# Equal tile offsets, scaled states on two engines, and products that fill TensorE's waits

## The chip, the cores and the metric

The kernel runs on one core of one Trainium2 chip. The metric is the device time of one execution in microseconds (us); the core has five engines, named as the profile names them: PE (TensorE matmul; PEld is its weight load), DVE (VectorE), ACT (ScalarE), POOL (GpSimd) and SP (SyncE, which here only issues DMAs).

## What is computed

Three stages, each feeding the next, all in float32 at the inputs and outputs:

```python
# gated linear attention, 4 batches x 8 heads, 768 steps, head size 48
for t in range(S):
    state = alpha[:, :, t, :, None] * state + einsum('bhd,bhe->bhde', k[:, :, t], v[:, :, t])
    y[:, :, t] = einsum('bhd,bhde->bhe', q[:, :, t], state)
x = y.transpose(0, 2, 1, 3).reshape(3072, 384)
# first feed-forward, 384 -> 2048 -> 384
h = x @ w_in;  x = (h * cos(h)) @ w_out
# second feed-forward, 384 -> 768 -> 384
h = maximum(maximum(x @ w1, x @ w2), x @ w3);  out = h @ w_out2
```

## The kernel before

The 3072 tokens are cut into six units of 512 (`u`). Attention (`att`) works a unit in four pairs of heads (`p`, processed as `k` = 0 to 3), and cuts 512 steps into eight chunks of 64. In a pair, POOL and DVE scale k and q by running products of alpha; TensorE transposes k (`trans`, L387), multiplies k with q and k with v (`akmm`, L399 and L404); ACT copies the k-q scores out (`a`, L411) and POOL masks them (L412); DVE carries the state from chunk to chunk (`state`, L421 and L423). TensorE then adds two parts into the output: scores by v (L449) and "scaled states" `d` by q (L455). A scaled state is a chunk's state times one column of `g`: in the first unit ACT makes it, one chunk and one head at a time (L430, 14 of them in a pair); in the later units POOL makes it, one head and all eight chunks at a time (L435, 2 in a pair). ACT copies the result out in two halves (L470), and in the first unit TensorE subtracts that rounded copy and ACT writes the remainder (L473, L475).

The first feed-forward, `moe1`, has 96 iterations, 16 blocks of hidden columns for each of six units. Each has 9 products that make h (L497 to L499) and 9 that multiply g into three accumulators (L524 to L526); a product streams 512 columns of a "moving" tile against a 128x128 stationary weight. Every number is held as a high and a low float32r part, so a float32 product takes three. The weights `wih`, `wil`, `woh`, `wol` are unpacked as they arrive: three DVE instructions a block (L310 to L312), one of ACT (L315) and one of POOL (L316). The second feed-forward, `moe2_h` (L574 to L576) and `moe2_o` (L597 to L599), is built of products of the same shape.

The order is not written by hand. Every step is recorded with an engine, an estimated duration, what it reads and writes, and a due time; `Program.order` simulates the engines and takes on each the earliest due step that is ready. Then the steps are issued in that order, each engine running its own list strictly in turn. So the estimated duration of one step can change the order of all.

The tiles lie in SBUF pools. The pool of attention's tiles (`ap`) starts at byte 73,856 of a partition. The pools of the feed-forward weights (`w1p`) and of the second feed-forward's hidden tiles (`np`) grow from the upper end, byte 229,344, downward. In the built program the tiles' first bytes, as remainders of a division by 64, are these:

| tile | before | after |
|---|---|---|
| moving tiles of `moe1`: `xt`, `gh`, `gl` | 0 | 0 |
| its weights `wih`, `wil`, `woh`, `wol` | 32 | 0 |
| `moe2_h`: moving `xt` / weights `w0`..`w2` | 0 / 0 | 0 / 0 |
| `moe2_o`: moving `h2` / weights `wo2` | 32 / 32 | 0 / 0 |
| attention's `kq` / `d` / `v`, `a`, `kt` | 32 / 0 / 0 | 0 / 0 / 0 |

Of the kernel before, what the change touches and what calls it, by code (L numbers as in the profile page):

```python
# [9 lines left out]
F32 = mybir.dt.float32  # L10
# [3 lines left out]
AF = mybir.ActivationFunctionType  # L14
# [4 lines left out]
B, H, S, D = 4, 8, 768, 48  # L19
# [4 lines left out]
P = 128  # L24
C = 64
HB = 512
NC = HB // C
# [4 lines left out]
C1 = C + 1  # L32
AL = NC * C1
# [14 lines left out]


NQ, NG, NRAW, NIN, NV, NGS = 3, 2, 3, 3, 2, 3  # L50
NBANK = 5
LIMIT = {"h": 3, "a": 3, "t": 1, "w": 1, "r": 2, "y": 2, "r0": 4}

# [9 lines left out]
MKP = 1  # L63

DAC = 1


W1E = 10
# [5 lines left out]


WARM, COLD, IDLE = 16, 7.0, 2.5


class Program:
# [15 lines left out]
    def op(self, eng, dur, fn, reads=(), writes=(), due=0.0, nbytes=None, port=False):  # L95
        n = len(self.ops)
        deps = set()
        for k in reads:
            if k in self.last_write:
                deps.add(self.last_write[k])  # L100
        for k in writes:
            if k in self.last_write:
                deps.add(self.last_write[k])
            deps.update(self.readers.get(k, ()))
        for k in writes:
            self.last_write[k] = n
            self.readers[k] = []
        for k in reads:
            self.readers.setdefault(k, []).append(n)
        for k in {*reads, *writes}:  # L110
            if isinstance(k, tuple) and k[0] == "ps":
                self.of_bank.setdefault(k, []).append(n)
        deps.discard(n)
        port = port or (eng == "Pool" and nbytes is None)
        self.ops.append((eng, dur, nbytes, fn, sorted(deps), due, port))
        return n

    def order(self, banks, limit):
        n = len(self.ops)
        left = [len(o[4]) for o in self.ops]  # L120
        users = [[] for _ in range(n)]
        for i, o in enumerate(self.ops):
            for d in o[4]:
                users[d].append(i)
        opens = {}
        bank_of = [[] for _ in range(n)]
        open_left = {}
        for k, v in self.of_bank.items():
            opens.setdefault(min(v), []).append(k)
            open_left[k] = len(v)  # L130
            for i in v:
                bank_of[i].append(k)
        bank_free = [0.0] * banks
        freed_at = {c: [0.0] * limit[c] for c in limit}
        bank_end = {}
        chosen = {}
        engines = sorted({o[0] for o in self.ops})
        free = dict.fromkeys(engines, 0.0)
        waiting = {e: [] for e in engines}
        ready_at = [0.0] * n  # L140
        for i in range(n):
            if not left[i]:
                waiting[self.ops[i][0]].append(i)
        start = [0.0] * n
        dma_free = 0.0
        port_free = 0.0
        cold = COLD
        never = float("inf")

        def single(t):  # L150
            return min(range(banks), key=lambda m: (bank_free[m] > t, bank_free[m], m))

        def ready(i):
            t = ready_at[i]
            need = opens.get(i, ())
            if need:

                t = max(t, sorted(freed_at[need[0][1]])[len(need) - 1], sorted(bank_free)[len(need) - 1])
            if self.ops[i][6]:
                t = max(t, port_free)  # L160
            return t

        for _ in range(n):
            t, e = min((max(free[e], min(map(ready, w))), e) for e, w in waiting.items() if w)
            assert t < never
            i = min((self.ops[j][5], j) for j in waiting[e] if ready(j) <= t)[1]
            waiting[e].remove(i)
            _, dur, nbytes, _, _, _, port = self.ops[i]
            start[i] = t
            if e == "PE":  # L170
                if t - free[e] > IDLE:
                    cold = t + COLD
                dur += min(dur, max(0.0, cold - t) / 2)
            free[e] = t + dur
            end = t + dur
            if port:
                port_free = end
            if nbytes is not None:
                dma_free = max(dma_free, end + (0.65 if e == "SP" else 1.05)) + nbytes / 260e3
                end = dma_free + 0.9  # L180
            for k in opens.get(i, ()):
                f = min(range(limit[k[1]]), key=lambda f: freed_at[k[1]][f])
                m = single(t)
                chosen[k] = m
                bank_end[k] = (m, f, 0.0)
                freed_at[k[1]][f] = never
                bank_free[m] = never
            for k in bank_of[i]:
                m, f, last = bank_end[k]
                last = max(last, end + self.SEM)  # L190
                bank_end[k] = (m, f, last)
                open_left[k] -= 1
                if not open_left[k]:
                    freed_at[k[1]][f] = last
                    bank_free[m] = last
            for u in users[i]:
                lag = self.LAG.get((e, self.ops[u][0]), self.SEM)
                ready_at[u] = max(ready_at[u], end + lag)
                left[u] -= 1
                if not left[u]:  # L200
                    waiting[self.ops[u][0]].append(u)
        self.start = start
        return sorted(range(n), key=lambda i: (start[i], i)), chosen


def act(n, psum=False):
    return (0.05 if psum else 0.095) + 0.00084 * n
# [33 lines left out]
def tile_kernel(ctx, tc, qka, vv, wt, outT):  # L241
# [18 lines left out]
    wi = {n: wp.tile([P, NF1, NR, P], F32R, name=f"wi{n}") for n in "hl"}  # L260
    wo = {n: wp.tile([P, NF1, DM], F32R, name=f"wo{n}") for n in "hl"}

    q_b = [mp.tile([P, HB], F32, name=f"q{i}") for i in range(NQ)]
    gh_b = [mp.tile([P, HB], F32R, name=f"gh{i}") for i in range(NG)]
    gl_b = [mp.tile([P, HB], F32R, name=f"gl{i}") for i in range(NG)]
# [2 lines left out]
    acc = [pp.tile([P, HB], F32, name=f"acc{i}") for i in range(NR)]  # L268
    ps_b = [pp.tile([P, 512], F32, name=f"ps{i}") for i in range(NBANK)]

    one0 = ap.tile([PR, NC, C1], F32, name="one0")
    inv0 = [ap.tile([PR, NC, C1], F32, name=f"inv{i}") for i in range(2)]
    tri = ap.tile([P, 1, C], F32, name="tri")
    al_b = [ap.tile([PR, KO], F32, name=f"al{i}") for i in range(NIN)]
    kq_b = [ap.tile([PR, 2 * HB], F32, name=f"kq{i}") for i in range(NIN)]
    g_b = [ap.tile([PR, AL], F32, name=f"g{i}") for i in range(NGS)]
    v_b = [ap.tile([P, N2, 2, UP], F32, name=f"v{i}") for i in range(NV)]
    kt_b = [ap.tile([P, N2, PR], F32, name=f"kt{i}") for i in range(2)]
    a_b = [ap.tile([P, 2, N2, C], F32, name=f"a{i}") for i in range(2)]
# [57 lines left out]
    def att(u, k, p, t0):  # L337
# [87 lines left out]
        for c in range(NC - 1):  # L425
            op("DVE", 0.2, lambda c=c: state(c), [rk[c % 2], *kgs, (*sk, c)], [(*sk, c + 1)], t0 + 0.25)
            if u < DAC and not firsts[c + 1]:
                for j in range(2):
                    w = slice(UP * j, UP * j + D)
                    op("Act", act(D) + 0.09, lambda c=c, j=j, w=w: se.activation(d[w, j, c + 1], s[w, c + 1], AF.Copy, scale=g[w, c + 1, 0:1]),  # L430
                       [*kgs, (*sk, c + 1)], [(dk, j, c + 1)], t0 + 0.25)
        if u >= DAC:
            for j in range(2):
                w = slice(UP * j, UP * j + D)
                op("Pool", pool(NC * D), lambda j=j, w=w: ge.tensor_tensor(d[w, j], s[w], g[w, :, 0:1].to_broadcast([D, NC, D]), ALU.mult),  # L435
                   [*kgs, *[(*sk, c) for c in range(NC)]], [(dk, j, c) for c in range(NC)], t0 + 0.25)
        elif not firsts[0]:
            for j in range(2):
                w = slice(UP * j, UP * j + D)
                op("Act", act(D) + 0.09, lambda j=j, w=w: se.activation(d[w, j, 0], s[w, 0], AF.Copy, scale=g[w, 0, 0:1]), [*kgs, (*sk, 0)], [(dk, j, 0)], t0 + 0.25)  # L440
        op("DVE", 0.2, lambda: state(NC - 1), [rk[1], *kgs, (*sk, NC - 1)], [(*sk, 0)], t0 + 0.27)

        yks, y = ([("acc", 0), ("acc", 1)], acc[:2]) if u == 0 else psum2("r" if u <= RYS else "y")
# [103 lines left out]
    def open_np():  # L547
        s_w1.close()
        np_ = ctx.enter_context(tc.tile_pool(name="np", bufs=1, side="right"))
        w2t["h2"] = [np_.tile([P, NF2, 2, HB], F32R, name=f"h2_{i}") for i in range(2)]  # L550
        w2t["t"] = [np_.tile([P, HB], F32, name=f"t2_{i}") for i in range(2)]
        w2t["y"] = [np_.tile([P, HB], F32, name=f"y2_{i}") for i in range(2)]
        for n in "hl":
            w2t["o" + n] = np_.tile([P, NF2, DM], F32R, name=f"wo2{n}")

    def x2_in(u, t0):
        n = u % 2
# [131 lines left out]
    build()  # L689
    order, chosen_ = G.order(NBANK, LIMIT)  # L690
    chosen.update(chosen_)
    build()
    with tc.manual_schedule():
        for i in order:
            G.ops[i][3]()


# [62 lines left out]
```

## Time and profile before

| | |
|---|---|
| time, median of 3 runs | 831.05 us (829.34 to 832.0) |
| the profiled execution | 831.06 us, its span 829.3 us |
| busy in the span | PE 805.4, DVE 477.7, ACT 372.5, POOL 189.0 us |
| TensorE's mean granted clock | 0.979 of full |

The span runs from the first to the last profiled instruction. A busy PE is not PE at its peak: matmuls are pipelined, and their recorded durations overlap. The distance from start to start tells the pace.

### The profile page before, as it was taken

The numbers are of one execution on the slowest core, as the hardware profiler recorded it, in microseconds if no ns is written. First come the engines' busy times: TensorE is split into PE (matmuls) and PEld (weight loads), VectorE is DVE, ScalarE is ACT, GpSimd is POOL, SyncE is SP. The second block draws the span as 40 slices with busy tenths as digits, with TensorE's granted clock in tenths as the row PEclk, the third lists the DMA queues.
The fourth block names the chain that finished last, engine by engine and source line by source line (L and its number), as shares of the span: only waits on it lengthen the run. The fifth ranks groups of instructions, "written<-read, shape, count | busy, mean of one in ns | idle before, by whom it ended". The sixth has DMA issues, their size and how long they took to land.

```text
span 829.3 us, 15144 instructions
## 1 busy us (share of the span) xinstructions
PE 805.4 (97%) x6168; PEld 649.1 (78%) x6168; DVE 477.7 (58%) x924; ACT 372.5 (45%) x695; POOL 189.0 (23%) x187
## 2 busy tenths in 40 slices
PE   7689999999999999999999999999999999999998
PEld 6567777878778877887788778888888888888886
DVE  7689999875786577657679954453122222322221
ACT  5865655645555554556466745521121211112121
POOL 6478777621231023102033200110000000000000
PEclk8589999999999999999999999999999999999999
DMA  9446764330242024102224610232020020200001
GB/s 281 137 133 193 208 188 150 117 106 12 73 146 65 1 76 143 43 1 74 65 86 134 238 45 2 104 106 77 26 88 19 22 89 25 77 26 13 13 26 38
DMA packets 26661, 71.86 MB, mean 87 GB/s; under 512 B 3488, under 2 KB 3488, under 8 KB 26592
## 3 DMA queue, kind: packets, MB, share of 16 engines
q1 hardware_dynamic: 26592, 70.90, 26.9%
q8 instruction: 48, 0.79, 0.4%
q14 instruction: 21, 0.17, 0.1%
HBM read 54.37 MB, written 14.16 MB: 83 GB/s over the span
## 4 chain that ended last, share of the span: by engine, by line
PE 84%; DVE 5%; POOL 4%; issue 3%; DMA 2%; ACT 1%; SPq 0%; DVEq 0%; POOLq 0%; ACTq 0%
PE ps L575 9%; PE ps L576 9%; PE ps L574 9%; PE acc L524 8%; PE acc L526 7%; PE ps L497 7%; PE acc L525 7%; PE ps L499 7%; PE ps L498 7%; PE ps L599 3%; PE ps L598 3%; PE ps L597 3%; PE ps L455 2%; PE ps L449 1%; PE ps L399 1%
## 5 line engine op out<-in xcount | busy, mean ns | idle before, releaser
L497 PE MATMUL ps<-xt,wih 128*128 128x512 f32 x288 | 117.7, 409 | 2.8 <-ACT q L506 1.7
L524 PE MATMUL acc<-gh,woh 128*128 128x512 f32 x288 | 117.5, 408 | 0.3 <-DVE yy L534 0.2
L499 PE MATMUL ps<-xt,wil 128*128 128x512 f32 x288 | 115.0, 399 | 1.4 <-POOL wil L316 1.4
L526 PE MATMUL acc<-gl,woh 128*128 128x512 f32 x288 | 114.4, 397 | 0.6 <-DVE gl L519 0.4
L498 PE MATMUL ps<-xt,wih 128*128 128x512 f32 x288 | 114.8, 399 | 0.0
L525 PE MATMUL acc<-gh,wol 128*128 128x512 f32 x288 | 114.0, 396 | 0.0
L504 ACT ACTIVATE q<-ps 128x512 int32<-128x512 f32 x96 | 57.2, 596 | 70.8 <-PE ps L499 70.2
L584 DVE TENSOR_TENSOR ps<-t,ps 128x512 f32<-128x512 f32 x36 | 25.0, 695 | 104.8 <-PE ps L576 104.7
L513 DVE SCALAR_TENSOR_TENSOR ps<-q,ps 128x512 f32<-128x512 f32 x76 | 52.7, 693 | 55.4 <-ACT q L507 55.2
L506 ACT ACTIVATE q<-q 128x512 f32<-128x512 f32 x96 | 60.6, 631 | 50.3 <-DVE q L505 49.6
L505 DVE SCALAR_TENSOR_TENSOR q<-q,ps 128x512 f32<-128x512 int32 x96 | 65.8, 685 | 28.0 <-ACT q L504 24.8
L585 ACT ACTIVATE h<-ps 128x512 fp32r<-128x512 f32 x36 | 21.5, 598 | 113.1 <-DVE ps L584 113.0
L519 DVE TENSOR_TENSOR gl<-ps,gh 128x512 fp32r<-128x512 f32 x76 | 52.1, 685 | 26.4 <-ACT gh L514 26.2
L497 PEld LDWEIGHTS ps<-xt,wih 128*128 128x128 f32 x288 | 54.6, 189 | 16.2 <-ACT q L506 2.2
L499 PEld LDWEIGHTS ps<-xt,wil 128*128 128x128 f32 x288 | 54.6, 190 | 15.3 <-POOL wil L316 2.1
L524 PEld LDWEIGHTS acc<-gh,woh 128*128 128x128 f32 x288 | 54.2, 188 | 15.0 <-DVE yy L534 1.1
L582 DVE TENSOR_TENSOR t<-t,ps 128x512 f32<-128x512 f32 x36 | 24.7, 687 | 71.4 <-PE ps L576 70.7
L526 PEld LDWEIGHTS acc<-gl,woh 128*128 128x128 f32 x288 | 54.2, 188 | 14.6 <-DVE gl L519 0.8
L514 ACT ACTIVATE gh<-ps 128x512 fp32r<-128x512 f32 x76 | 45.3, 597 | 42.8 <-DVE ps L513 39.9
L498 PEld LDWEIGHTS ps<-xt,wih 128*128 128x128 f32 x288 | 54.8, 190 | 11.8
L525 PEld LDWEIGHTS acc<-gh,wol 128*128 128x128 f32 x288 | 54.3, 189 | 11.7
L435 POOL TENSOR_TENSOR d<-s,g 48x384 f32<-48x384 f32 x40 | 34.6, 864 | 122.7 <-DVE s L423 121.1
(122 smaller groups left out, 1595.2 us busy)
## 6 DMA issues: line engine op xcount, KB each, us to landing
raw<-in_wt SPq DMA_DIRECT2D x56, 384.0 KB, 3.4
kq<-in_qka SPq DMA_DIRECT2D x23, 448.0 KB, 4.5
x1d<-yy SPq DMA_DIRECT2D x18, 512.0 KB, 2.8
xt<-x1d SPq DMA_DIRECT2D x18, 512.0 KB, 4.3
v<-in_vv SPq DMA_DIRECT2D x22, 256.0 KB, 3.5
al<-in_qka SPq DMA_DIRECT2D x24, 228.4 KB, 3.0
outT<-y SPq DMA_DIRECT2D x18, 256.0 KB, 2.0
xt<-yy SPq DMA_DIRECT2D x36, 64.0 KB, 2.7
```

Source lines behind the costliest of these rows:

```text
L497: pe.matmul(ps, wi["h"][:, f, cc], xt[:, cc, 0], start=(cc == 0), stop=False)
L498: pe.matmul(ps, wi["h"][:, f, cc], xt[:, cc, 1], start=False, stop=False)
L499: pe.matmul(ps, wi["l"][:, f, cc], xt[:, cc, 0], start=False, stop=(cc == NR - 1))
L504: op("Act", act(HB, True), lambda: se.activation(q.bitcast(I32), ps, AF.Copy, scale=INV2PI), [hk], [qk], m)
L505: op("DVE", dve(HB), lambda: ve.scalar_tensor_tensor(q, q.bitcast(I32), -TWOPI, ps, ALU.mult, ALU.add), [hk], [qk], m)
L506: op("Act", act(HB), lambda: se.activation(q, q, AF.Sin, scale=0.5), (), [qk], m)
L524: pe.matmul(acc[c], oh, gh, start=(f == 0), stop=False)
L525: pe.matmul(acc[c], ol, gh, start=False, stop=False)
L526: pe.matmul(acc[c], oh, gl, start=False, stop=(f == NF1 - 1))
L574: pe.matmul(ps, w2t["h"][m][:, f, cc], xt[:, cc, 0], start=(cc == 0), stop=False)
L575: pe.matmul(ps, w2t["h"][m][:, f, cc], xt[:, cc, 1], start=False, stop=False)
L576: pe.matmul(ps, w2t["l"][m][:, f, cc], xt[:, cc, 0], start=False, stop=(cc == NR - 1))
```

## The change

Three things change. (1) Attention's tiles `one0`, `inv`, `al` and `g` get lines of 544 floats (2,176 bytes) in place of 520 or 522, of which the same part is used as before, and a tile of 88 floats (352 bytes) is added in each of the two pools that grow from the upper end; this moves tiles to the offsets of the table above. (2) In the first unit ACT makes the scaled states of one head of a pair, as before, and POOL those of the other, in one instruction for all chunks; the planner's estimate of ACT's instruction rises by 0.12 us. (3) The planner keeps, for each TensorE step, the idle time that it foresees before it (`gap`). In front of steps planned to start before 48 us that open a bank of PSUM, and in front of `values`, the program issues up to ten products of the identity with itself, one for each 0.22 us of that gap above 0.3 us. They write to the bank that the step behind them overwrites.

```diff
+PAD = 88
+LINE = 544
+DAH = 1
+FILL, NFILL, SPARE = 48.0, 10, 0.3
...
             if e == "PE":
+                gap[i] = t - free[e]
...
+    wp.tile([P, PAD], F32, name="pad")
...
-    one0 = ap.tile([PR, NC, C1], F32, name="one0")
+    one0 = ap.tile([PR, LINE], F32, name="one0")[:, 0:AL].rearrange("p (c t) -> p c t", c=NC)
-    al_b = [ap.tile([PR, KO], F32, name=f"al{i}") for i in range(NIN)]
+    al_b = [ap.tile([PR, LINE], F32, name=f"al{i}")[:, 0:KO] for i in range(NIN)]
-    g_b = [ap.tile([PR, AL], F32, name=f"g{i}") for i in range(NGS)]
+    g_b = [ap.tile([PR, LINE], F32, name=f"g{i}")[:, 0:AL] for i in range(NGS)]
...
             if u < DAC and not firsts[c + 1]:
-                for j in range(2):
+                for j in range(DAH):
                     w = slice(UP * j, UP * j + D)
-                    op("Act", act(D) + 0.09, lambda c=c, j=j, w=w: se.activation(d[w, j, c + 1], s[w, c + 1], AF.Copy, scale=g[w, c + 1, 0:1]),
+                    op("Act", act(D) + 0.21, lambda c=c, j=j, w=w: se.activation(d[w, j, c + 1], s[w, c + 1], AF.Copy, scale=g[w, c + 1, 0:1]),
...
-        if u >= DAC:
-            for j in range(2):
+        for j in range(2):
+            if u >= DAC or j >= DAH:
                 w = slice(UP * j, UP * j + D)
                 op("Pool", pool(NC * D), lambda j=j, w=w: ge.tensor_tensor(d[w, j], s[w], g[w, :, 0:1].to_broadcast([D, NC, D]), ALU.mult),
...
+        np_.tile([P, PAD], F32, name="pad2")
...
         for i in order:
+            if G.ops[i][0] == "PE" and plan.start[i] < FILL:
+                bank = ps_b[chosen[plan.opens[i][0]]] if i in plan.opens else acc[0] if G.ops[i][3].__name__ == "values" else None
+                for _ in range(min(NFILL, int((plan.gap[i] - SPARE) / 0.22)) if bank is not None else 0):
+                    pe.matmul(bank[:, 0:P], ident, ident, start=True, stop=True)
             G.ops[i][3]()
```

The line numbers of the changed file are 10 or 11 higher from attention on. ACT's list from the first pair's scores to the third pair's, before (kt is the transposed k, a the scores, d the scaled states, yy and xt the output's two parts; the number behind a name is its buffer):

```order
L411 ACTIVATE a_119<-ps_98 128x256
L430 ACTIVATE d_125<-s_124,g_112 48x48 x4
L390 ACTIVATE kt_118<-ps_100 128x448
L430 ACTIVATE d_125<-s_124,g_112 48x48 x6
L411 ACTIVATE a_120<-ps_97 128x256
L430 ACTIVATE d_125<-s_124,g_112 48x48 x4
L411 ACTIVATE a_120<-ps_101 128x256
L390 ACTIVATE kt_117<-ps_100 128x448
L430 ACTIVATE d_126<-s_121,g_113 48x48 x7
L470 ACTIVATE yy_89<-acc_94 128x256
L470 ACTIVATE yy_89<-acc_95 128x256
L430 ACTIVATE d_126<-s_121,g_113 48x48 x4
```

The same stretch of ACT's list now:

```order
L422 ACTIVATE a_120<-ps_100 128x256
L441 ACTIVATE d_126<-s_125,g_113 48x48 x2
L401 ACTIVATE kt_119<-ps_101 128x448
L441 ACTIVATE d_126<-s_125,g_113 48x48 x3
L422 ACTIVATE a_121<-ps_102 128x256
L422 ACTIVATE a_121<-ps_98 128x256
L441 ACTIVATE d_126<-s_125,g_113 48x48 x2
L441 ACTIVATE d_127<-s_122,g_114 48x48 x7
L401 ACTIVATE kt_118<-ps_101 128x448
L480 ACTIVATE yy_90<-acc_95 128x256
L480 ACTIVATE yy_90<-acc_96 128x256
L422 ACTIVATE a_120<-ps_100 128x256
```

Ahead of the second pair's first score copy stood ten scaled states and between its two copies four; now it is five and none, and a score copy of the third pair (the last row) comes directly behind the output copies. POOL's list from the first pair's mask on, before:

```order
L412 TENSOR_TENSOR a_119<-a_119,tri 128x256 x2
L367 TENSOR_TENSOR kq_111<-kq_111,g_114 112x512
L412 TENSOR_TENSOR a_120<-a_120,tri 128x256
L382 TENSOR_TENSOR kq_111<-kq_111,al_108 112x512
L412 TENSOR_TENSOR a_120<-a_120,tri 128x256
L412 TENSOR_TENSOR a_119<-a_119,tri 128x256 x2
L367 TENSOR_TENSOR yy_90<-yy_90,g_112 112x512
L316 TENSOR_TENSOR wil<-raw_91,wih 128x384
L382 TENSOR_TENSOR yy_90<-yy_90,al_106 112x512
```

and now:

```order
L423 TENSOR_TENSOR a_120<-a_120,tri 128x256 x2
L378 TENSOR_TENSOR kq_112<-kq_112,g_115 112x512
L446 TENSOR_TENSOR d_126<-s_125,g_113 48x384
L393 TENSOR_TENSOR kq_112<-kq_112,al_109 112x512
L423 TENSOR_TENSOR a_121<-a_121,tri 128x256 x2
L446 TENSOR_TENSOR d_127<-s_122,g_114 48x384
L423 TENSOR_TENSOR a_120<-a_120,tri 128x256 x2
L327 TENSOR_TENSOR wil<-raw_92,wih 128x384
L327 TENSOR_TENSOR wol<-raw_93,woh 128x384
L378 TENSOR_TENSOR yy_91<-yy_91,g_113 112x512
L446 TENSOR_TENSOR d_126<-s_123,g_115 48x384
L393 TENSOR_TENSOR yy_91<-yy_91,al_107 112x512
```

Three of the four new scaled-state instructions (L446) stand here, and two weight blocks come ahead of the fourth pair's k (`yy`). TensorE's list at the end of the fourth pair's k-v products, before:

```order
L404 MATMUL ps_97<-q_84,kt_118 48x48
L473 MATMUL acc_95<-xt_463,minus 128x256
L497 MATMUL ps_99<-xt_463,wih 128x512
L498 MATMUL ps_99<-xt_463,wih 128x512
L499 MATMUL ps_99<-xt_463,wil 128x512
```

and now:

```order
L415 MATMUL ps_101<-q_85,kt_119 48x48
L483 MATMUL acc_95<-xt_466,minus 128x256
L483 MATMUL acc_96<-xt_466,minus 128x256
L711 MATMUL ps_99<-ident 128x128 x10
L507 MATMUL ps_99<-xt_466,wih 128x512
L508 MATMUL ps_99<-xt_466,wih 128x512
L509 MATMUL ps_99<-xt_466,wil 128x512
```

Ten filling products (L711) stand ahead of the first product of `moe1`. In all there are 37, at eleven places: 2, 5, 4, 1, 1, 2, 4, 1, 10, 5 and 2.

## Rows read from the trace of the kernel before

**Rows 1.** The page: the granted TensorE clock in 40 slices of 20.7 us.

```profile
PEclk8589999999999999999999999999999999999999
```

**Rows 2.** Windows: stretch, its us, busy PE, PEld, DVE, ACT, POOL, clock, DMA, GB/s.

```profile
0.00:10.00 10.00, 7.62 (x100) 7.29 (x100) 8.07 (x18) 2.14 (x3) 7.64 (x18) 1.00 0.84 254
10.00:30.00 20.00, 14.08 (x280) 11.68 (x284) 14.18 (x46) 18.64 (x57) 8.84 (x10) 0.58 0.75 221
30.00:52.00 22.00, 17.10 (x269) 12.97 (x262) 16.65 (x34) 12.96 (x36) 15.67 (x14) 0.61 0.51 138
60.00:150.00 90.00, 85.68 (x931) 67.40 (x931) 85.64 (x185) 55.68 (x105) 67.39 (x59) 1.00 0.58 174
150.00:545.00 395.00, 394.36 (x3347) 314.47 (x3346) 273.09 (x524) 223.05 (x397) 81.36 (x79) 1.00 0.27 84
560.00:820.00 260.00, 260.00 (x1142) 213.98 (x1141) 65.68 (x95) 47.19 (x79) 0.00 (x0) 1.00 0.11 41
```

**Rows 3.** Timeline of PE, 484 to 524 us: first and last of 172 rows.

```profile
483.79 0.39 PE L498 MATMUL ps<-xt,wih 128*128 128x512 f32 x1
...
523.86 0.40 PE L498 MATMUL ps<-xt,wih 128*128 128x512 f32 x1
```

**Rows 4.** Timeline of PE, 700 to 740 us: first and last of 177 rows.

```profile
699.80 0.39 PE L598 MATMUL ps<-h,wo2l 128*128 128x512 f32 x1
...
739.92 0.39 PE L574 MATMUL ps<-xt,w2h 128*128 128x512 f32 x1
```

**Rows 5.** Groups by line, PE, 150 to 545 us: count | busy us, mean ns | idle before.

```profile
L524 PE MATMUL acc<-gh,woh 128*128 128x512 f32 x239 | 97.2, 407 | 0.3 <-DVE yy L534 0.2
...
L497 PE MATMUL ps<-xt,wih 128*128 128x512 f32 x229 | 92.7, 405 | 0.0
```

**Rows 6.** Timeline of PE, 13 to 45 us: attention's `d` by `q` products.

```profile
30.69 1.73 PE L455 MATMUL acc<-kq,d 112*48 112x64 f32 x28
42.25 1.69 PE L455 MATMUL acc<-yy,d 112*48 112x64 f32 x28
```

**Rows 7.** Waits of DVE, 0 to 52 us: total us, times, longest.

```profile
DVE s L423 <- ACT a L411: 5.5, 4, 2.8
DVE s L421 <- ACT a L411: 5.0, 2, 4.5
```

**Rows 8.** Timeline, 18.4 to 24.6 us: start, us, what [idle before].

```profile
18.50 1.04 PE L404 MATMUL ps<-q,kt 64*64 64x48 f32 x32
...
20.61 1.40 ACT L430 ACTIVATE d<-s,g 48x48 f32<-48x48 f32 x4
...
22.57 1.04 ACT L430 ACTIVATE d<-s,g 48x48 f32<-48x48 f32 x3
23.64 0.66 ACT L411 ACTIVATE a<-ps 128x256 f32<-128x256 f32 x2
...
24.33 0.26 DVE L423 SCALAR_TENSOR_TENSOR s<-s,g,ps 112x48 f32<-112x48 f32 x1 [2.76 <-ACT a L411]
```

**Rows 9.** The chain that ended last, 30 to 40 us: start, us, what.

```profile
31.31 2.00 POOL wil L316
33.31 1.15 POOL yy L382
...
34.50 1.13 PE ps L399 x32
35.63 0.81 PE ps L404 x28
36.44 0.53 PE acc L473
```

**Rows 10.** By line (L430, L435, L423): ns min/median/max, first and last start; idle before L423.

```profile
L430 ACT ACTIVATE d<-s,g x56: 325/331/336, 10.8 to 42.2; 48x48 f32<-48x48 f32 x56
...
L435 POOL TENSOR_TENSOR d<-s,g x40: 835/845/1662, 53.9 to 416.5; 48x384 f32<-48x384 f32 x40
...
  POOL d L435: 0.2, 1
```

**Rows 11.** Timeline at the start: the 16 warm-up products, two records each.

```profile
1.43 6.11 PE L639 MATMUL acc<-ident 128*128 128x128 f32 x32 [1.43 <-POOL ident masks.py:199]
```

More of the change, by code (lines that the diff above doesn't have):

```diff
@@ L144, in order @@
         start = [0.0] * n
+        gap = [0.0] * n
         dma_free = 0.0
@@ L202, in order @@
         self.start = start
+        self.gap = gap
+        self.opens = opens
         return sorted(range(n), key=lambda i: (start[i], i)), chosen
@@ L269, in tile_kernel @@
     ps_b = [pp.tile([P, 512], F32, name=f"ps{i}") for i in range(NBANK)]
-    one0 = ap.tile([PR, NC, C1], F32, name="one0")
-    inv0 = [ap.tile([PR, NC, C1], F32, name=f"inv{i}") for i in range(2)]
+    one0 = ap.tile([PR, LINE], F32, name="one0")[:, 0:AL].rearrange("p (c t) -> p c t", c=NC)
+    inv0 = [ap.tile([PR, LINE], F32, name=f"inv{i}")[:, 0:AL].rearrange("p (c t) -> p c t", c=NC) for i in range(2)]
     tri = ap.tile([P, 1, C], F32, name="tri")
-    al_b = [ap.tile([PR, KO], F32, name=f"al{i}") for i in range(NIN)]
+    al_b = [ap.tile([PR, LINE], F32, name=f"al{i}")[:, 0:KO] for i in range(NIN)]
     kq_b = [ap.tile([PR, 2 * HB], F32, name=f"kq{i}") for i in range(NIN)]
-    g_b = [ap.tile([PR, AL], F32, name=f"g{i}") for i in range(NGS)]
+    g_b = [ap.tile([PR, LINE], F32, name=f"g{i}")[:, 0:AL] for i in range(NGS)]
     v_b = [ap.tile([P, N2, 2, UP], F32, name=f"v{i}") for i in range(NV)]
@@ L436, in att @@
                    [*kgs, *[(*sk, c) for c in range(NC)]], [(dk, j, c) for c in range(NC)], t0 + 0.25)
-        elif not firsts[0]:
-            for j in range(2):
+            elif not firsts[0]:
                 w = slice(UP * j, UP * j + D)
-                op("Act", act(D) + 0.09, lambda j=j, w=w: se.activation(d[w, j, 0], s[w, 0], AF.Copy, scale=g[w, 0, 0:1]), [*kgs, (*sk, 0)], [(dk, j, 0)], t0 + 0.25)
+                op("Act", act(D) + 0.21, lambda j=j, w=w: se.activation(d[w, j, 0], s[w, 0], AF.Copy, scale=g[w, 0, 0:1]), [*kgs, (*sk, 0)], [(dk, j, 0)], t0 + 0.25)
         op("DVE", 0.2, lambda: state(NC - 1), [rk[1], *kgs, (*sk, NC - 1)], [(*sk, 0)], t0 + 0.27)
@@ L691, in tile_kernel @@
     chosen.update(chosen_)
+    plan = G
     build()
```

## Prediction

> **What bounds the kernel now.** I read the windows first, since the share of busy time over the whole span mixes three stages. From 150 us to the end TensorE is never idle: 394.36 of 395 us, then 260 of 260 [rows 2]. There only the pace of its products counts. From 60 to 150 us it shares the bound with VectorE: 85.68 and 85.64 of 90 us busy [rows 2], since VectorE still unpacks weights and scans the second unit's alpha. Before 52 us nobody is full: VectorE is busy 8.07 + 14.18 + 16.65 = 38.9 of 52 us, TensorE 7.62 + 14.08 + 17.10 = 38.8, and ScalarE is at 18.64 of 20 us from 10 to 30 [rows 2]. TensorE's granted clock shows digits of 8, 5 and 8 in the first three slices and is full from the fourth [rows 1]; over 10 to 30 and 30 to 52 us it averages 0.58 and 0.61 [rows 2], a mix of its two levels, 1.2 and 2.4 GHz.
>
> Two waits in this first part matter. VectorE stood 5.5 + 5.0 = 10.5 us waiting for ScalarE's copies of the scores [rows 7]. One of them shows how: the third pair's products were issued at 18.50 and took 1.04 us, so they were done at 19.5, but the copy began at 23.64, behind seven scaled states (4 in 1.40 us, 3 in 1.04 us) and the output's copies; VectorE idled 2.76 us ahead of its next state [rows 8]. The largest, 4.5 us, has another chain behind it: GpSimd unpacks a weight for 2.00 us, then scales the fourth pair's q, and only then can TensorE start its products at 34.50, which take 1.13 + 0.81 + 0.53 = 2.47 us at the lower clock [rows 9].
>
> **Offsets.** I compare the pace of the same product in two stages. In `moe1` 171 steps from start to start take 523.86 − 483.79 = 40.07 us, 234.3 ns each [rows 3]. In the second feed-forward 176 steps take 739.92 − 699.80 = 40.12 us, 228.0 ns each [rows 4]; 260 us with 1142 products give 227.7 [rows 2]. Shapes, types and clock are the same, and neither stretch has an idle moment. What differs is where the operands lie: in `moe1` the moving tile starts at a multiple of 64 bytes and the weights 32 past one, while in the second feed-forward both remainders are equal, 0 and 0 or 32 and 32. After the change they are 0 and 0 everywhere. If that is the reason, each `moe1` product falls by 234.3 − 228.0 = 6.3 ns. From 150 to 545 us there are three groups like L524's with 239 products each and three like L497's with 229 or 230, 1405 in all [rows 5], and TensorE is the bound: 1405 × 6.3 ns = 8.9 us. From 60 to 150 us stand another 291 of the 1728, worth 1.8 us; VectorE and TensorE bind there in turn, so I take half, 0.9 us, with 0 and 1.8 as its ends.
>
> A second reading fits the same rows: in `moe1` the moving tile lies in the lower part of SBUF and the weights in the upper, while in the other stage both lie on one side. Then the offsets would give nothing. I choose the first as much the likelier: the 40 us of the second feed-forward mix products whose operands lie low at remainder 0 with such as lie high at remainder 32, both kinds keep the one pace [rows 4], and so neither the side nor the remainder itself has a price there; no row shows one for distance.
>
> The Trainium skill speaks against this term: "TensorE: Matmul & The Clock Gate", Part 2 (Step-by-step), says that TensorE reads moving operand and weights through two ports of its own, so that loading the next weights takes no read bandwidth from the running product. By that rule the pace would not hang on offsets and this term would be 0 in place of 9.8 us; the trace does not settle it, but shows two paces that the rule has no place for.
>
> Attention's float32 products get nothing. In the first unit the fourth pair's q lay at remainder 0, like its `d`, the other pairs' at 32: the 28 records took 1.69 and 1.73 us [rows 6], and the earlier of them lay wholly in the lower clock, the later not quite. Scans, masks and DMAs keep sizes and counts; the offsets of their tiles I cost at 0.
>
> **Scaled states.** ScalarE loses 28 of its 56 instructions at 0.331 us [rows 10], 9.3 us, most of it where it is full. GpSimd gains four at 0.845 us, up to 1.66 when a VectorE scan holds it up [rows 10]: 3.4 to 6.6 us. GpSimd is busy 7.64 + 8.84 + 15.67 = 32.2 of 52 us [rows 2], so there is room, but each now stands ahead of k and q scalings in its list. They also bring a wait: the instruction reads all eight chunks, so VectorE's last state of the pair, which overwrites the first chunk, waits for it, and the next states and weights queue behind. In the later units the same pattern made VectorE wait 0.2 us, once [rows 10]; I cost it at 0, at worst 4 × 0.845 = 3.4 us.
>
> What it brings is what vanishes of the 10.5 us: VectorE is the scarce engine as far as 150 us, so what it does earlier ends the stage earlier. The copies that ScalarE's queue made late go nearly all; the 4.5 us are due to GpSimd and TensorE as well, and GpSimd's list now has two weight blocks ahead of the fourth pair. I take half, 5.2 us, with ends of 0 and 10.5.
>
> **Filling products.** There are 37. The 16 warm-up products took 6.11 us, 0.38 us each [rows 11]: 37 × 0.38 = 14.1 us at most. TensorE idles 52 − 38.8 = 13.2 us in this part, and the products stand only where the planner foresees idling, so I cost them at 0, with 14.1 us as the other end if every one delays the step behind it. They may hold the clock up. Of that only what lies on the chain counts: the 2.47 us of the fourth pair would halve [rows 9], 1.2 us. The clock fell before although TensorE was busy 14.08 of 20 us [rows 2], so I take half, 0.6 us.
>
> **Sum.** 8.9 + 0.9 + 5.2 + 0.6 = 15.6 us off the profiled execution's 831.06 us, which is the median of the runs (831.05): 815.4 us. With the ends of the terms (0 to 1.8, 0 to 10.5, 0 to 1.2 us, some filling on the path) this case runs from 808 to 822 us.
>
> **Rivals.** First, offsets don't matter, by distance or because the stage itself is slower: for it speaks that rows show only two stages, not one tile moved; against it that the slow pace holds in a stretch without DMAs, scans or waits. Then 831.06 − 5.2 − 0.6 = 825.3 us. By the skill's rule on two read ports this is what should come.
>
> Second, the offsets work and the first unit gives nothing: GpSimd, with more to do and in turn, or the filling products take ScalarE's place, and VectorE waits as long for something else. The row of GpSimd's 2.00 us weight [rows 9], twice the usual, speaks for it; the room of 20 us against it. Then 831.06 − 9.8 = 821.3 us.
>
> Third, slower: the filling products stand on the path. TensorE works strictly in turn, so a step whose input arrives sooner than planned waits for all of the fill ahead of it; ten before the first product of `moe1` alone are 3.8 us. If all 37 delay what follows and no other gain of the first part survives, 831.06 + 14.1 − 9.8 = 835.4 us. It decides from 9.8 us on the path, 26 of the 37 products. Against it: they stand behind the inputs' own waits, of which there are 13.2 us.
>
> **How the numbers follow.** My forecast gets 0.68, the first rival 0.14, the second 0.13, the third 0.05. A difference within 0.3% (2.5 us) is about what a measurement of this kernel cannot tell from no change. Slower by more is most of the third, 0.03; its milder forms and a first rival whose first unit gives little end within, 0.03; all else is faster, 0.94. For 8 in 10 I reach from 808, the forecast's low end, to 825, just short of the first rival.
>
> **What would show it.** In the changed profile, offsets: `moe1` from 480 us on should step at 227 to 228 ns where it was 234; if it stays at 234, the reading is wrong and I lose most of the sum. Scaled states: VectorE's waits for the score copies should fall from 10.5 to about 5 us, and the first dense run of `moe1` should start some 5 us before 52; a new wait of VectorE for GpSimd's `d` would show the second rival. Fill: the clock between 10 and 45 us, and whether the steps behind L711 start when their inputs arrive or when the fill ends. If 60 to 150 us takes as long as before at a faster pace, VectorE alone was the bound there, and the 0.9 us are gone.

## The result and the profile after

The changed kernel takes 819.58 us (median; 816.63 to 821.03) where the kernel before took 831.0 us (829.34 to 832.0) beside it: the ratio is 0.986, with a 95% interval of 0.9825 to 0.9895. The forecast was 815.4 us with a range of 808 to 825. The profiled execution took 820.76 us, with a span of 819.0 us.

The page's clock line answers to [rows 1]:

```profile
PEclk9889999999999999999999999999999999999999
```

The three low digits 8, 5 and 8 have become 9, 8 and 8. The windows answer to [rows 2]; their columns are those given there.

```profile
0.00:10.00 10.00, 8.12 (x104) 7.88 (x104) 7.23 (x16) 2.14 (x3) 6.75 (x18) 1.00 0.84 232
10.00:30.00 20.00, 16.17 (x324) 14.22 (x328) 17.56 (x50) 13.09 (x41) 15.45 (x17) 0.84 0.90 245
30.00:52.00 22.00, 17.16 (x302) 14.25 (x295) 17.04 (x40) 8.85 (x25) 17.54 (x15) 0.92 0.69 204
60.00:150.00 90.00, 85.81 (x937) 68.45 (x936) 84.91 (x184) 53.07 (x103) 69.73 (x60) 0.99 0.56 170
150.00:545.00 395.00, 393.92 (x3382) 319.78 (x3381) 275.55 (x526) 225.99 (x401) 79.27 (x79) 1.00 0.26 84
```

Read three things here. The clock of the two early stretches rose from 0.58 and 0.61 to 0.84 and 0.92. VectorE is busier from 10 to 30 us, 17.56 us against 14.18, and ScalarE freer, 13.09 against 18.64. From 150 us on TensorE does 3382 instructions in the 395 us where it did 3347, while it is as full as before.

The timeline of PE from 479.9 to 520.1 us, first and last of 179 rows (in `moe1`, and a few products of the second feed-forward at its end), answers to [rows 3]:

```profile
479.69 0.39 PE L536 MATMUL acc<-gl,woh 128*128 128x512 f32 x1
...
520.04 0.39 PE L585 MATMUL ps<-xt,w1h 128*128 128x512 f32 x1
```

178 steps take 40.35 us, 226.7 ns each, where the step was 234.3 ns. From 699.9 to 740.1 us, first and last of 179 rows, as in [rows 4]:

```profile
699.56 0.39 PE L585 MATMUL ps<-xt,w0h 128*128 128x512 f32 x1
...
739.91 0.39 PE L586 MATMUL ps<-xt,w2h 128*128 128x512 f32 x1
```

This is 226.7 ns as well; it was 228.0.

Where the time came from is read from marks inside `moe1`: the last product of its 17th iteration (the 51st at that line) and of its 96th (the 288th). The timeline of PE of the kernel before has them at

```profile
152.47 0.40 PE L526 MATMUL acc<-gl,woh 128*128 128x512 f32 x1
...
535.25 0.39 PE L526 MATMUL acc<-gl,woh 128*128 128x512 f32 x1
```

and that of the changed kernel at

```profile
152.76 0.39 PE L536 MATMUL acc<-gl,woh 128*128 128x512 f32 x1
...
526.61 0.39 PE L536 MATMUL acc<-gl,woh 128*128 128x512 f32 x1
```

At 152 us the changed kernel is 0.3 us behind. Between the marks it gains 382.78 − 373.85 = 8.9 us, and the span as a whole is 829.3 − 819.0 = 10.3 us shorter, so 1.7 us more come behind the last mark. Of the 8.9 us, 1.7 belong ahead of the first mark: the changed kernel has 64 small attention products fewer between the marks (1771 steps among them, 36.8 us, against 1835 in 38.5), since it did them earlier. So in this execution the dense products' pace gives some 9 us and the first 150 us about 1.4.

The first unit itself, up to 52 us, went better than that. VectorE's waits from 0 to 52 us, which answer to [rows 7]:

```profile
DVE s L432 <- ACT a L422: 3.6, 2, 2.8
DVE s L434 <- ACT a L422: 1.4, 3, 0.7
```

The waits for score copies fell from 10.5 to 5.0 us. GpSimd's scalings took 842 ns each (median), and in this stretch VectorE waited for none of them; its one wait for `d`, 0.3 us, stands in a later unit, at 236.6 us. But TensorE's timeline shows what came behind:

```profile
44.01 0.85 PE L483 MATMUL acc<-xt,minus 128*128 128x256 f32 x2 [0.40 <-ACT xt L480]
44.66 0.63 PE L507 MATMUL ps<-xt,wih 128*128 128x512 f32 x1
...
46.79 0.63 PE L509 MATMUL ps<-xt,wil 128*128 128x512 f32 x1
47.23 1.44 PE L711 MATMUL ps<-ident 128*128 128x128 f32 x10
48.51 0.55 PE L398 MATMUL ps<-ident,kq 112*128 112x112 f32 x4
49.76 0.71 PE L711 MATMUL ps<-ident 128*128 128x128 f32 x4 [0.69 <-ACT kt L401]
50.22 0.48 PE L507 MATMUL ps<-xt,wih 128*128 128x512 f32 x1
...
53.49 0.39 PE L509 MATMUL ps<-xt,wil 128*128 128x512 f32 x1
56.92 0.57 PE L398 MATMUL ps<-ident,kq 112*128 112x112 f32 x4 [3.04 <-DVE raw L323]
57.42 0.64 PE L507 MATMUL ps<-xt,wih 128*128 128x512 f32 x1
```

The fourth pair's last products (L483) were issued at 44.01. Then six `moe1` products ran at the lower clock (a step of 0.43 us); five filling products (two records each) stood ahead of the transposes at 48.51, and two more ahead of the next `moe1` product, which starts at 50.22 us. At 53.9 us TensorE then stands for 3.04 us: the wait ahead of the transposes ends with VectorE's weight unpacking (L323), which had used a PSUM bank until then, and when TensorE goes on, its clock is at the lower level again. In the kernel before, the same transposes wait 2.00 us.

### The profile page after: what moved, and what is told of

Same layout as the page of the kernel before. It is cut to its first block, busy times and chain, and to the rows that moved or that the text cites. A ratio compares the mean times of both kernels' runs of the same rounds, so it can differ in the third digit from the quotient of the medians.

```text
span 819.0 us, 15259 instructions
## 1 busy us (share of the span) xinstructions
PE 796.5 (97%) x6242; PEld 651.7 (80%) x6242; DVE 476.6 (58%) x924; ACT 360.6 (44%) x667; POOL 193.3 (24%) x191
## 4 chain that ended last, share of the span: by engine, by line
PE 85%; DVE 6%; POOL 2%; issue 2%; DMA 2%; ACT 2%; SPq 0%; POOLq 0%; DVEq 0%; ACTq 0%
PE ps L585 9%; PE ps L587 9%; PE ps L586 9%; PE acc L534 7%; PE ps L507 7%; PE acc L536 7%; PE acc L535 7%; PE ps L508 7%; PE ps L509 7%; PE ps L608 3%; PE ps L610 3%; PE ps L609 3%; PE ps L465 2%; PE ps L410 1%; PE ps L459 1%
## 5 line engine op out<-in xcount | busy, mean ns | idle before, releaser
L507 PE MATMUL ps<-xt,wih 128*128 128x512 f32 x288 | 115.9, 403 | 1.7 <-ACT kt L401 1.5
L508 PE MATMUL ps<-xt,wih 128*128 128x512 f32 x288 | 113.4, 394 | 0.0
L509 PE MATMUL ps<-xt,wil 128*128 128x512 f32 x288 | 113.3, 393 | 0.0
L446 POOL TENSOR_TENSOR d<-s,g 48x384 f32<-48x384 f32 x44 | 37.1, 842 | 124.8 <-DVE s L434 123.1
L509 PEld LDWEIGHTS ps<-xt,wil 128*128 128x128 f32 x288 | 54.8, 190 | 11.8
```

The source lines that it names most:

```text
L507: pe.matmul(ps, wi["h"][:, f, cc], xt[:, cc, 0], start=(cc == 0), stop=False)
L508: pe.matmul(ps, wi["h"][:, f, cc], xt[:, cc, 1], start=False, stop=False)
L509: pe.matmul(ps, wi["l"][:, f, cc], xt[:, cc, 0], start=False, stop=(cc == NR - 1))
```

## The experiments

Each kernel ran beside the kernel before, whose medians in these runs were 830.98 to 831.79 us.

**Offsets alone.** The kernel before with the offsets of the change and nothing else.

```diff
+PAD = 88
+LINE = 544
+    wp.tile([P, PAD], F32, name="pad")
-    al_b = [ap.tile([PR, KO], F32, name=f"al{i}") for i in range(NIN)]
+    al_b = [ap.tile([PR, LINE], F32, name=f"al{i}")[:, 0:KO] for i in range(NIN)]
...
+        np_.tile([P, PAD], F32, name="pad2")
```

> The kernel before with the offsets alone (the lines of 544 floats and both pads), scaled states and order as before. Theory A (the offsets set the pace): the first feed-forward's products step at 227 ns in place of 234 and the time falls by about 10 us, to 820-822. Theory B (the place in SBUF or the stage sets it): 234 ns stay and the time is 830-832.

Measured: 821.37 us (819.02 to 822.75), ratio 0.9873 (0.9852 to 0.9895), 10.2 us less. The pace of `moe1` is 226.7 ns. The two marks of before stand in its timeline at

```profile
151.84 0.39 PE L529 MATMUL acc<-gl,woh 128*128 128x512 f32 x1
...
526.82 0.39 PE L529 MATMUL acc<-gl,woh 128*128 128x512 f32 x1
```

It is 0.6 us ahead at the first and 8.4 at the second: 7.8 us between them, with as many attention products as before (1835 steps, 38.5 us), and 1.7 us behind the second (spans 829.3 and 819.2). The offsets carry nearly the whole result. Up to 150 us their 7.6 ns a product bring nothing that shows: from 60 to 150 us TensorE did 929 instructions where it had done 931 [rows 2]. VectorE was busy for 84.84 of these 90 us and may have been the bound; the 0.6 us at the first mark cannot be told from the scatter, since two runs below that keep the slow pace are 0.4 and 1.3 us ahead there.

**No filling products.** The changed kernel with

```diff
-FILL, NFILL, SPARE = 48.0, 10, 0.3
+FILL, NFILL, SPARE = 0.0, 10, 0.3
```

> The changed kernel without the filling products, all else as changed. Theory F1 (the fill takes back what the split gains: seven filling products between 47 and 50 us and the wait behind them): 815-817. Theory F2 (the fill holds the clock up and pays): slower than the changed kernel's 819.6 by 1 to 3 us, 821-823. Theory F3 (VectorE sets the end of the stage at 150 us, TensorE's waits do not matter): 819-821.

Measured: 818.89 us (816.4 to 819.59), ratio 0.9841 (0.982 to 0.9862): the same as the changed kernel within what can be told, and between the times that the three theories named. Against the offsets alone it is 2.5 us less, and that is what the split is worth without the fill.

**No split.** The changed kernel with both halves of the first unit's scaled states on ScalarE, as before, but with the change's raised estimate for them (0.21 us over the copy where it was 0.09).

```diff
-DAH = 1
+DAH = 2
```

> The changed kernel with both heads' scaled states on ScalarE again in the first unit (the raised estimate stays, the filling products follow its own plan). If the split is worth the 5.2 us of the prediction: 824-826. If what it gives is used up before 150 us: 819-821.

Measured: 828.03 us (827.05 to 828.78), ratio 0.9955 (0.9939 to 0.997). This is 8.5 us slower than the changed kernel and 6.7 us slower than the offsets alone: far more than any theory here had put on the split. Something besides the split had to be in it.

**Old offsets.** The changed kernel with the tiles where they were.

```diff
-    wp.tile([P, PAD], F32, name="pad")
-    al_b = [ap.tile([PR, LINE], F32, name=f"al{i}")[:, 0:KO] for i in range(NIN)]
+    al_b = [ap.tile([PR, KO], F32, name=f"al{i}") for i in range(NIN)]
...
-        np_.tile([P, PAD], F32, name="pad2")
```

> The changed kernel with the old offsets, split and fill as changed; its instructions and their order are those of the changed kernel. By the prediction's sum: 831.0 less 5.2 and 0.6, so 825. If split and fill together give nothing, as iteration 16 of the first feed-forward says (152.5 us before, 152.8 after): 830-832, with the pace at 234 ns.

Measured: 827.46 us (826.93 to 828.95), ratio 0.9952 (0.9933 to 0.997). From 479.9 to 520.1 us its `moe1` products step at 234.3 ns again. The time lies between the two that were expected: split and fill together are worth 831.53 − 827.46 = 4.1 us here, the offsets 7.9 us on top of them.

**Neither split nor fill**, with the raised estimate: the changed kernel with DAH = 2 and FILL = 0.0.

> The changed kernel without split and without fill: the offsets and the raised estimate of ScalarE's scaled states are all that is left. If the fill made the run without split 6.6 us slower than the offsets alone (828.0 against 821.4): 820-823. If the order that the raised estimate gives did it: 826-829.

Measured: 827.58 us (827.0 to 830.67), ratio 0.9966 (0.9954 to 0.9977). Without the split the fill changes nothing (828.03 against 827.58). The only difference to the offsets alone is the estimate, and it costs 6.2 us, through the order that the planner makes of it. TensorE's waits from 0 to 62 us show how such an order loses time:

```profile
PE acc L459 <- POOL a L423: 6.7, 6, 2.8
PE ps L507 <- DVE raw L323: 3.0, 1, 3.0
PE ps L507 <- DMA xt<-yy: 2.9, 1, 2.9
```

The scores now wait for GpSimd's masks and two `moe1` products for weights and a transfer; none of the three is among the long waits of the run with the offsets alone.

**The first twenty filling products only**: the changed kernel with FILL = 30.0.

> The changed kernel with only the first 20 filling products, those planned before 30 us; the 17 around the first products of the first feed-forward are gone. If those 17 take back what the split gives: 816-818.5, below the run without fill or equal to it. If VectorE alone sets the end of this stage: 818-820, no different from with or without fill.

Measured: 815.29 us (813.04 to 817.58), ratio 0.9813 (0.9793 to 0.9833), 4.3 us less than the changed kernel and 3.6 us less than without any fill. The early fill helps, and something among the 17 late ones takes that back.

**The weights 32 bytes further.** The kernel before with one unused tile of 8 floats behind the first experts' weights, so that these start 64 past a multiple of 128 bytes, where the moving tiles are at 0: equal within 64 bytes, as the prediction had asked, but not within 128.

```diff
+    wp.tile([P, 8], F32, name="pad")
```

> The kernel before with one tile of 8 floats added behind the first feed-forward's weights, which moves these by 32 bytes, to a multiple of 64 but not of 128, and nothing else that a product reads. Theory A (agreement within 64 bytes): these products step at 227 ns, about 9 us off, 821-823. If agreement within 128 is needed, or the place in SBUF decides (theory B): 234 ns, 830-832. The second feed-forward keeps its pace of 228 ns.

Measured: 828.88 us (828.0 to 830.44), ratio 0.9979 (0.997 to 0.9989). PE's timeline from 479.9 to 520.1 us, first and last of 174 rows:

```profile
479.60 0.40 PE L526 MATMUL acc<-gh,wol 128*128 128x512 f32 x1
...
519.97 0.39 PE L525 MATMUL acc<-gh,woh 128*128 128x512 f32 x1
```

40.37 us for 173 steps are 233.4 ns. Agreement within 64 bytes is not what it takes.

**Fill on the old plan.** The run with the offsets alone plus the filling products where its own plan foresees idling (33 of them), without the split and with the old estimate.

> The offsets and the filling products on the order of the kernel before (33 of them by its plan), no split, old estimate. If the fill costs what it delays: 823-826 against the offsets' 821.4. If it is hidden: 820-822. If the held clock pays: 818-820.

Measured: 820.40 us (819.98 to 822.02), ratio 0.9878 (0.9864 to 0.9892): 1.0 us less than the offsets alone, which is within what these runs can tell. So the whole fill brings nothing that shows without the split, as all 37 products bring nothing with it (818.89 without them, 819.58 with). Whether its early part alone would gain without the split wasn't tried.

**The weights 480 bytes further.** As two runs above, with 120 floats: weights and moving tiles both start at multiples of 128 bytes, but 128 apart in each 256.

> The kernel before with an unused tile of 480 bytes a partition behind the experts' first weights in their pool, and nothing else. The weights of moe1 then start at multiples of 128 bytes, as the moving states do, but at another remainder of 256 than these: the run with the weights 32 bytes further on (remainder 64 of 128, moving at 0) stepped 233.4 ns and took 828.88 us, the run with the offsets of the change (equal up to 512) 226.7 ns and 821.37 us. Theory that operands must agree up to 128 bytes: moe1 steps about 227 ns and the time is 820 to 823 us, as with the change's offsets. Rival, agreement is needed up to 256 bytes or more: the step stays at 230 to 234 ns and the time is 828 to 831 us.

Measured: 828.88 us (827.46 to 831.92), ratio 0.9972 (0.9958 to 0.9985). PE's timeline from 479.9 to 520.1 us, first and last of 174 rows:

```profile
479.68 0.39 PE L527 MATMUL acc<-gl,woh 128*128 128x512 f32 x1
...
519.88 0.40 PE L499 MATMUL ps<-xt,wih 128*128 128x512 f32 x1
```

173 steps in 40.20 us, 232.4 ns: still the slow pace, so 128 bytes are not enough either.

**The weights 96 bytes further.** The same with 24 floats, so that weights and moving tiles are at the same place in each 256 bytes, though 256 apart in each 512.

```diff
+    wp.tile([P, 24], F32, name="pad")
```

> The kernel before with an unused tile of 96 bytes a partition behind the experts' first weights, and nothing else: the weights of moe1 then start 256 bytes apart from the moving states in each 512, at the same place in each 256. With weights and states 128 apart in each 256 (480 bytes added) the step was 232.5 ns and the time 828.88 us; with both at the same place in each 512 (the offsets of the change) the step was 226.7 ns and the time 821.37 us. Theory that agreement up to 256 bytes is enough: moe1 steps about 227 to 228 ns and the time is 821 to 823.5 us, since only the second experts' 1.5 us and the attention's offsets are missing. Rival, agreement is needed up to 512: the step is 230 to 234 ns and the time 827 to 831 us.

Measured: 821.65 us (821.02 to 822.96), ratio 0.9886 (0.9869 to 0.9904). PE's timeline from 479.9 to 520.1 us, first and last of 179 rows:

```profile
479.68 0.39 PE L498 MATMUL ps<-xt,wih 128*128 128x512 f32 x1
...
520.02 0.39 PE L526 MATMUL acc<-gh,wol 128*128 128x512 f32 x1
```

178 steps in 40.34 us, 226.6 ns. One unused tile of 96 bytes a partition gives 9.3 of the 10.2 us that all the offsets gave. The offsets inside the attention's pool, which make up most of that part of the diff, are worth nothing that shows; the second experts' weights are the likely rest, since from 700 to 740 us the pace stays at 228.1 ns here.

**Fill up to the first `moe1` product**: the changed kernel with FILL = 36.0, thirty filling products; the last five and two are left out.

> The changed kernel with the products that are overwritten up to 36 us of the plan: the first twenty and the ten that stand ahead of the first dense moe1 product, without the last five and two in front of the transposes and the kt copy. With twenty the time was 815.29 us, with all 37 it was 819.58 us, so the last 17 cost 4.3 us. Theory that the seven at 47 to 50 us cost it, because they stand between the first unit's attention and the first moe1 product: 815 to 816 us, and the first dense moe1 product at about 46 us of the span. Rival, the ten cost it: 818 to 820 us, with the first dense product at 49 us or later. Rival, both share it: 816.5 to 818 us.

Measured: 815.74 us (811.81 to 817.92), ratio 0.9804 (0.9779 to 0.9828), as with the first twenty. So the ten ahead of the first `moe1` product cost nothing that shows. In this execution that product still waits 1.60 us behind them for a transfer of xt. In the profiled execution of the changed kernel it starts right behind the fill, at 34.87 us, but the chain that ended last runs through VectorE there, from 33.80 to 43.13 us. PE's timeline of this run:

```profile
28.05 2.40 PE L711 MATMUL ps<-ident 128*128 128x128 f32 x20
32.05 0.50 PE L507 MATMUL ps<-xt,wih 128*128 128x512 f32 x1 [1.60 <-DMA xt<-yy]
...
39.51 0.85 PE L483 MATMUL acc<-xt,minus 128*128 128x256 f32 x2 [0.41 <-ACT xt L480]
...
42.30 0.60 PE L509 MATMUL ps<-xt,wil 128*128 128x512 f32 x1
42.78 0.57 PE L398 MATMUL ps<-ident,kq 112*128 112x112 f32 x4
44.04 0.50 PE L507 MATMUL ps<-xt,wih 128*128 128x512 f32 x1 [0.69 <-ACT kt L401]
...
50.80 0.57 PE L398 MATMUL ps<-ident,kq 112*128 112x112 f32 x4 [3.03 <-DVE raw L323]
```

From the start of the sixth product (L509) to the next `moe1` product it is 1.74 us, against 50.22 − 46.79 = 3.43 us in the changed kernel: the seven late products cost 1.7 us on the chain directly. (The dense run starts at 44.04 us, where some 46 was expected.) The chain of the changed kernel has them, at their lengths on it, 1.25 and 0.71 us:

```profile
47.42 1.25 PE ps L711 x10
...
49.76 0.71 PE ps L711 x4
```

The medians of the runs with twenty and with thirty lie 4.3 and 3.8 us below that of the changed kernel, and the other 2 us are not explained by the seven. The program ahead of them is the same in both, and yet L483 was issued at 39.51 us in the one profiled execution and at 44.01 us in the other.

**The old estimate with the split**: the changed kernel without fill and with 0.09 us again.

```diff
-                    op("Act", act(D) + 0.21, lambda c=c, j=j, w=w: ...
+                    op("Act", act(D) + 0.09, lambda c=c, j=j, w=w: ...
-FILL, NFILL, SPARE = 48.0, 10, 0.3
+FILL, NFILL, SPARE = 0.0, 10, 0.3
```

> The changed kernel without its filling products and with the estimate for ScalarE's scaled states put back to what it was before (0.09 instead of 0.21 us over the copy), so that only offsets and split are left. With the raised estimate this was 818.89 us. Without the split the raised estimate cost 6.2 us (827.58 against 821.37 us with the offsets alone). Theory that the estimate's price hangs on the longer ScalarE chain of the unsplit form: here within 1.5 us of 818.89 us. Rival, the estimate costs whatever the split: 814 to 816.5 us here, and then the split by itself is worth 5 us or more. Rival, the estimate is needed with the split: 821 us or more, and the split alone is worth nothing.

Measured: 818.11 us (816.64 to 819.02), ratio 0.9837 (0.9817 to 0.9857). With the split the estimate makes no difference (818.89); its 6.2 us hang on the unsplit form. So the split is worth 2.5 to 3.3 us over the offsets alone.

Put in a row of medians: 831 us before; 821.4 with the offsets; 818.1 to 818.9 with the split; 815.3 to 815.7 with the first twenty or thirty filling products; 819.6 with all 37. The versions with 20 and 30 beat both kernels.

## Why the prediction was right, and where not

The direction, the range and the main term held, and the point was 4.2 us too low. That the offsets' 9.8 us meet 10.2 measured is partly luck: 8.9 and 0.9 were forecast where 7.8 and nothing came, and 1.7 came where nothing was forecast.

**Offsets in `moe1`: 8.9 us forecast, 7.8 measured, from a partly wrong reading.** The 7.8 us lie between the marks of the run with the offsets alone, 79 iterations of 18 products, 5.5 ns each. The forecast's 6.3 ns came from the stretch of [rows 3], which shows more than the average (there it was even 234.3 − 226.7 = 7.6). What is missing stands behind attention's small products: between the marks of the run with the offsets alone, the second to the sixth step behind each group of them still average 230 to 233 ns, and 226.7 comes back at about the twelfth. That the pace hangs on how the operands lie is shown: moving nothing but the weights, by 96 bytes, took the step from 234.3 to 226.6 ns, and by 480 bytes only to 232.4. The rival that offsets don't matter falls. The Trainium skill says in "TensorE: Matmul & The Clock Gate", Part 2 (Step-by-step), that loading weights takes no read bandwidth from the running product. The trace does not agree as far as the pace goes: the two runs differ in the place of the weights alone, and the measurement decides.

Wrong was the size that has to agree. The prediction compared remainders of 64; the run with 32 bytes (233.4 ns) and the one with 480 (232.4 ns) show that agreement within 64 or 128 bytes isn't enough and the one with 96 that 256 is. What the change needed it happened to give, since its tiles agree within 512. Nor does the weights' own place decide: in the second feed-forward of the kernel before, `wo2` started where the slow `moe1` weights did, 480 bytes past a multiple of 512 (both pools end at byte 229,344, and all their tiles are multiples of 512 long), but its moving tile `h2` did too, and its products reach the fast pace (lines below).

**The second feed-forward: costed at 0, worth 1.7 us.** Its step fell from 228.0 to 226.7 ns; 1296 products give 1.7 us, as the spans do behind the second mark. The prediction took this stage for free, because both kinds of products agree within themselves and seemed to keep one pace [rows 4]. But 228.0 is a mean of two paces. The tiles of `moe2_o` lay 480 bytes past a multiple of 512 and those of `moe2_h` 128 past one, and PE's timeline of the kernel before shows what a change from one kind to the other costs:

```profile
626.26 0.40 PE L597 MATMUL ps<-h,wo2h 128*128 128x512 f32 x1
...
628.35 0.39 PE L597 MATMUL ps<-h,wo2h 128*128 128x512 f32 x1
...
630.16 0.40 PE L599 MATMUL ps<-h,wo2h 128*128 128x512 f32 x1
630.40 0.39 PE L574 MATMUL ps<-xt,w2h 128*128 128x512 f32 x1
...
632.48 0.39 PE L574 MATMUL ps<-xt,w0h 128*128 128x512 f32 x1
...
635.88 0.39 PE L574 MATMUL ps<-xt,w1h 128*128 128x512 f32 x1
```

The first nine steps of `moe2_o` take 232 ns each, the next eight 226; then the first nine of `moe2_h` take 231, and the 15 behind them 226.7. Away from such a change both kinds step at 226.7 ns before as well, so the remainder itself has no price; after the change all four kinds of tiles start at the same place in each 512 bytes, and the slow steps are gone. Why there are nine of them no run shows. With 7.8 us this makes 9.5 of the 10.2 us.

**60 to 150 us: 0.9 us forecast, nothing came that shows.** The sign that the prediction named was whether this stretch takes as long as before at the faster pace; with the offsets alone it does, 929 instructions for 931.

**Split: 5.2 us forecast, 2.5 to 3.3 us measured.** The wait that was meant to go went as forecast (10.5 to 5.0 us), and no wait for GpSimd's `d` took its place. The step that was too large is the next one, that what VectorE does earlier ends the stage earlier by as much. In the changed kernel VectorE was busy 41.8 of the first 52 us (7.23 + 17.56 + 17.04) where it had been 38.9, the dense run of `moe1` began at 50.22 us where it had begun at 51.96, and at 152 us about 1.4 us was left. Without the fill more arrives. PE's timeline of that run has the start of the dense run and the first mark at

```profile
47.42 0.50 PE L507 MATMUL ps<-xt,wih 128*128 128x512 f32 x1 [0.69 <-ACT kt L401]
...
148.40 0.39 PE L536 MATMUL acc<-gl,woh 128*128 128x512 f32 x1
```

4.5 and 4.1 us ahead of the kernel before, with VectorE busy 44.2 of the first 52 us. That is nearly what was forecast, but this execution was the fastest of its four (816.4 us), and by the medians half is left. One part of the rest may be the 3.04 us stall at the transposes, which is in the runs with no, twenty and thirty fillings as well (3.03 to 3.04 us). The run with the old estimate has another order without that stall, but one of 3.3 us ahead of a `moe1` product, and takes the same time. So what the missing half went to stays open.

**Filling products: costed at 0 with a gain of 0.6 us.** Two terms of opposite sign stood behind that 0. The first twenty or thirty gained 3.2 to 3.6 us. In the run with thirty the granted clock from 10 to 30 us is full:

```profile
10.00:30.00 20.00, 18.10 (x444) 15.87 (x443) 17.90 (x54) 15.38 (x49) 16.20 (x18) 1.00 0.92 278
```

(These are the windows of the run with thirty.) With the same products there it is 0.91 in the run with twenty and 0.84 in the changed kernel; unfilled it is 0.59, and 0.73 with the old estimate. So the clock's term was probably too small: only the fourth pair's 2.47 us had been counted, while most of the first unit's attention runs in this stretch. The last seven cost 1.7 us directly and with it 3.8 to 4.3 us in the medians. This is the third rival's mechanism, at seven products in place of 26 and with a fraction of its price: the prediction took the ten ahead of the first `moe1` product as the dangerous ones, and those cost nothing that shows.

The second rival, that the first unit gives nothing, gave 821.3 us and comes near the profiled execution. One of its two causes was at work, the filling products, by the late seven. The other was not: VectorE did not wait for GpSimd's new scalings. TensorE waited 2.95 us, once, for a q that GpSimd scales (at 42.48 us), but the chain that ended last runs through VectorE there.

## What to carry to other kernels

Where dense products stand back to back and still step at two paces in two stages, compare where moving and stationary tiles start, here within 256 bytes, and move one of them with an unused tile; 96 bytes a partition took 1.1% off this kernel's time. Look at single steps too: a mean can hide a few slow ones behind each change from one pair of tiles to another. Fill a waiting TensorE only where the step behind it waits for something else anyway: look up, for each place, whether the next product starts when its input arrives or when the fill ends. And change an estimate that a planner uses as carefully as an instruction: here one number moved the time by 6.2 us, with no instruction added.

## What the runs showed of the hardware that was not expected

The step of a 128x512 float32r product with its own weight load was 234.3 ns with the weights 352 bytes past the moving tile's place in each 512, 233.4 at 320, 232.4 at 384, and 226.6 to 226.7 at 0 and at 256. Transfers don't set it: in the kernel before, the steps of `moe1` between 160 and 525 us average 234.0 ns while a DMA packet moves and 234.2 while none does. Where products of two such pairs take turns, it also hangs on the pair before: some nine steps behind each change were slow in the second feed-forward, though each product's own tiles agreed.

The time of the first unit varies between executions of the same instructions. In the two executions compared above the fourth pair's L483 came 4.5 us apart, and the five runs with thirty fillings spread over 6.1 us, where seventeen of the kernel before beside them spread over 4.2. TensorE's timeline of the changed kernel has, at 17.43 and 23.22 us, waits that nothing in the profile ends:

```profile
17.43 0.34 PE L459 MATMUL acc<-a,v 64*64 64x64 f32 x7 [1.20 <-issue]
...
23.22 0.49 PE L459 MATMUL acc<-a,v 64*64 64x64 f32 x12 [1.01 <-issue]
23.64 1.73 PE L465 MATMUL acc<-kq,d 112*48 112x64 f32 x28
```

With thirty fillings they are 0.72 and 0.19 us. Behind the second of them the clock is at the lower level in the one (28 products in 1.73 us) and at the full level in the other (0.99 us). What TensorE waited for there stays open.
